# Spreading the score tiles of an attention stage over the eight PSUM banks in another way

## The chip, the cores and the metric

The program runs on one core of a Trainium2 chip. The metric is the device time of one execution in microseconds (us). Five engines matter: TensorE (PE, with its weight loads shown as PEld), VectorE (DVE), ScalarE (ACT), GpSimd (POOL), and SyncE (SP), which here only issues DMA transfers. TensorE writes its results into PSUM, which has eight banks of 2 KB a partition; ACT and DVE read them from there.

## The reference

A transformer block over 2048 tokens of width 576, with a modulation computed from one vector `c`. What matters here is its first half:

```python
h = layernorm(x) * (1 + ca) + sa
q, k, v = split(h @ wqkv)                  # 32 heads of 18
scores = q @ k.T * 18 ** -0.5              # a query sees itself and the 255 keys before it
o = softmax(scores) @ v
x = x + ga * (o @ wo)
h = layernorm(x) * (1 + cb) + sb
x = x + gb * mixer_and_mlp(h)              # token shift with w1, w2; then w3 (576 to 4608), gelu, w4
```

## The kernel before

Nearly every product is made exact by splitting an operand into a rounded high part and the low part that is left; a tile's high part is copied out of PSUM by ACT, and DVE or POOL subtracts it to get the low part.

The work has three phases that follow each other. Phase A holds layernorm, q/k/v projection, attention and the first 12 tiles of the output projection. Phase B holds the last four of these and the token mixer, phase C the MLP. Phases B and C allocate their own PSUM pool and are untouched in it.

All steps of a phase are put on a time line by hand (`play` sorts them by a due time). In phase A the order of PE and POOL is exactly this order (`manual_schedule`); the order on ACT, DVE and SP is left to the framework's scheduler. A PSUM tile names a tag; tiles of one tag share `bufs` banks, and a new tile waits until the last reader of the bank's old tile is done. In phase A the eight banks are shared out as: `sc` 3, `st` 2, `tr` 2, `av` 1.

The steps of phase A that the change and the prediction touch:

- **Row transposes** (`tr` inside `ln`). A normalized row tile of 128 tokens is transposed in two PSUM tiles, `hT..pa` (512 columns, line 283) and `hT..pb` (the last 64 features, line 286). ACT applies scale and shift (lines 291, 293) and makes the high part (294, 295); POOL makes the low part of `pa` (296), DVE that of `pb` (297).
- **Projections** (`vproj`, `qproj`). 14 matmuls each into a tile from `dense`, which walks through `sc` and `st` in turn. q and k go to DRAM (`qkh`, `qkl`) and come back as unit loads.
- **Attention units.** There are 32: 4 chunks `c` of 8 heads, 4 groups `g` of 512 queries, 2 halves `hq` of 4 heads. `uload` brings a unit's q and k into one of four buffers `U` by 12 DMAs on SP (line 399). `s2` computes row-wise scores, 16 tiles `sc` (425), and DVE takes the row maximum of each (432); the maxima are transposed (446, tile `mT` in `tr`), copied by ACT (448) and written into the unit's `U` by two DMAs on SP (450). `s3` computes the scores again, transposed, with the maximum taken off: 16 tiles `X` in `st` (12 where g is 0), each one or two matmuls (475) and a mask matmul (476); ACT takes the exponential of each (482). Twice a unit the products with v follow (497, one `av` bank), and their result is copied (502), transposed (509, tile `oT` in `tr`), divided (511, 515) and written out (517). On PE, `s3` of one unit and `s2` of a later one alternate tile by tile.
- **Output projection** (`s4`, in phase A for g below 3 during chunk 3). A row tile is loaded, transposed by `split9` (lines 64 to 74: `oTT..pa` and `oTT..pb`, both in `tr`; DVE's low parts at 70 and 74), multiplied by `wo` in two halves (676, tiles `po` in `tr`), added (677), and normalized on DVE and POOL.
- **Modulation vectors** (`spill`, line 202): eight small matmul groups into `tr` during chunks 1 and 2.

Of the kernel before, what the change touches and what calls it, by code (L numbers as in the profile page):

```python
# [8 lines left out]
F32 = mybir.dt.float32  # L9
F32R = mybir.dt.float32r  # L10
# [40 lines left out]
class Kern:  # L51
# [11 lines left out]

    def split9(self, row, L, cs, name):
        nc = self.nc
        pa = self.ps.tile([P, KC, P], F32, tag="tr", name=name + "pa", bufs=self.b_tr)
        for k in range(KC):
            nc.tensor.transpose(pa[:, k, :], row[:, k * P:(k + 1) * P], self.ident)
        nc.scalar.copy(L[:, 0:KC, cs], pa)
        nc.vector.tensor_tensor(out=L[:, KC:2 * KC, cs], in0=pa, in1=L[:, 0:KC, cs].bitcast(F32), op=ALU.subtract)  # L70
        pb = self.ps.tile([TAIL, P], F32, tag="tr", name=name + "pb", bufs=self.b_tr)
        nc.tensor.transpose(pb, row[:, KC * P:D], self.ident)
        nc.scalar.copy(L[:TAIL, 2 * KC, cs], pb)
        nc.vector.tensor_tensor(out=L[TAIL:, 2 * KC, cs], in0=pb, in1=L[:TAIL, 2 * KC, cs].bitcast(F32), op=ALU.subtract)
# [52 lines left out]
    def phase_a(self):  # L127
# [8 lines left out]
        qkl = self.dr.tile([2 * D, S], F32, name="qkl")  # L136
        NGA = 4
        with ExitStack() as st:
            self.ps = self.pool(st, "psA", space=PSUM)
# [25 lines left out]
            def cond():  # L165
                fm["x"] = pp.tile([P, 12 * P], F32, tag="P", name="modx", bufs=self.b_p)
                cr = fm["x"][0:KC + 1, 9 * P:10 * P]
                sr = fm["x"][0:KC + 1, 10 * P:11 * P]
                nc.vector.memset(cr, 0.0)
                nc.sync.dma_start(cr[0:KC, :], self.c[0:1, 0:KC * P].rearrange("o (k p) -> (o k) p", p=P))  # L170
                nc.sync.dma_start(cr[KC:KC + 1, 0:TAIL], self.c[0:1, KC * P:])
                nc.scalar.activation(sr, cr, AF.Exp, scale=-1.0)
                nc.vector.tensor_scalar(sr, sr, 1.0, None, op0=ALU.add)
                nc.vector.reciprocal(sr, sr)
                nc.vector.tensor_tensor(out=sr, in0=sr, in1=cr, op=ALU.mult)
                pc = self.ps.tile([P, KC + 1], F32, tag="tr", name="pc", bufs=self.b_tr)
                nc.tensor.transpose(pc, sr, self.ident[0:KC + 1, 0:KC + 1])
                nc.vector.tensor_copy(silu, pc)

            def modvec(v):  # L180
# [17 lines left out]
                def spill():  # L198
                    for hf in range(2):
                        cs = slice(hf * 288, (hf + 1) * 288)  # L200
                        pm = self.ps.tile([P, 288], F32, tag="tr", name=f"pm{v}{hf}", bufs=self.b_tr)
                        nc.tensor.matmul(pm, ones, acc[0][:, cs], start=True, stop=True)
# [48 lines left out]
            def mod_tr():  # L251
                pc = self.ps.tile([P, 3, P], F32, tag="tr", name="pc2", bufs=self.b_tr)
                for j in range(2):
# [10 lines left out]
            def ln(t):  # L264
# [13 lines left out]
                def tr():  # L278
# [3 lines left out]
                    x, L, cs = xrows[t], hT[g], slice(i * P, (i + 1) * P)  # L282
                    pa = self.ps.tile([P, KC, P], F32, tag="tr", name=f"hT{t}pa", bufs=self.b_tr)
                    for k in range(KC):
                        nc.tensor.transpose(pa[:, k, :], x[:, k * P:(k + 1) * P], self.ident)
                    pb = self.ps.tile([TAIL, P], F32, tag="tr", name=f"hT{t}pb", bufs=self.b_tr)
                    nc.tensor.transpose(pb, x[:, KC * P:D], self.ident)
# [49 lines left out]

            banks_p = [("sc", self.b_sc), ("st", self.b_st), ("sc", self.b_sc), ("st", self.b_st), ("sc", self.b_sc)]
            turn = [0]
# [72 lines left out]
            def s2(c, g, hq):  # L412
# [29 lines left out]
                def fin2():  # L442
                    mr = box[1]
                    pm = self.ps.tile([8, 4, P], F32R, tag="tr", name=f"mT{c}_{g}_{hq}", bufs=self.b_tr)
                    for i in range(4):
# [8 lines left out]
            def s3(c, g, hq):  # L454
# [50 lines left out]
                def fin2():  # L505
                    avs = abox[1]
                    pt = self.ps.tile([P, 4, 4, 32], F32, tag="tr", name=f"oT{c}_{g}_{hq}", bufs=self.b_tr)
                    for i in range(4):
# [140 lines left out]
    def s4(self, g, i):  # L649
# [10 lines left out]
        def tr():  # L660
            box["T"] = rp.tile([P, 2 * KC + 1, P], F32R, tag="oT", name=f"oT{t}", bufs=1)
            self.split9(box["o"], box["T"], slice(0, P), f"oTT{t}")

        def wo(hf):
            def f():
                T, x = box["T"], box["x"]
                cs = slice(hf * 288, (hf + 1) * 288)
                tag = "tr" if g < 3 else "mm"
                po = self.ps.tile([P, 288], F32, tag=tag, name=f"po{t}_{hf}", bufs=self.b_tr if g < 3 else self.b_mm)
                pl = []  # L670
# [93 lines left out]
    def phase_bc(self):  # L764
        nc = self.nc
        with ExitStack() as st:
            cp = self.cp = self.pool(st, "bc")
            self.ps = self.pool(st, "psB", space=PSUM)
            self.gb = cp.tile([P, D], F32, name="gb")
            nc.sync.dma_start(self.gb, self.modd[5].to_broadcast([P, D]))  # L770
# [298 lines left out]
    ng = NG  # L1069
    b_mm, b_sc, b_st, b_tr, b_av = 1, 3, 2, 2, 1  # L1070
    b_row, b_p, b_xn, b_gf, b_x1 = 5, 4, 2, 2, 4
# [39 lines left out]
```

## Time and profile before

| | |
|---|---|
| median of 3 runs | 1833.42 us (1831.3 to 1837.96) |
| profiled execution, its time | 1839.11 us |
| its span in the profile | 1837.0 us |
| PE busy over the span | 1761.6 us (96%) |
| DVE, ACT, POOL busy | 984.2, 611.1, 385.6 us |
| row transposes and projections | about 19 to 236 us |
| attention, with output projection from 600 us on | about 206 to 735 us |
| phase B, then phase C | about 735 to 1837 us |

A row of a timeline reads: start, duration, engine, line, operation, output<-inputs, shape, count; in brackets how long the engine stood idle before it and what ended that. A row of the waits reads: who, where, whom it waited for; total us, times, longest. PE's durations are modelled and overlap, so the starts carry more than the lengths. A row of the windows reads: the stretch, its length, busy time (and count) of PE, PEld, DVE, ACT, POOL, the granted share of the TensorE clock, the DMA engines' busy share, GB/s.

### The profile page before, as it was taken

What the parts mean: (1) busy time and instruction counts of PE and PEld (TensorE: products, weight loads), DVE (VectorE), ACT (ScalarE), POOL (GpSimd) and SP (SyncE); (2) the same over time, 40 slices, a digit from 0 to 9 for tenths busy, and PEclk for the clock granted to TensorE, in tenths of its full rate; (3) what the DMA queues carried; (4) which work ended last, traced back from release to release, by engine and by line L of the source; (5) the groups of instructions that cost most, each with busy time, mean ns of one, the idle gap of its engine ahead of it and who ended that gap; (6) DMA issues with size and microseconds to landing.
All of it is one profiled execution on the core that took longest, in us unless ns stands there. A gap on an engine that the chain in (4) does not pass through costs nothing.

```text
span 1837.0 us, 30267 instructions
## 1 busy us (share of the span) xinstructions
PE 1761.6 (96%) x11700; PEld 1508.9 (82%) x11700; DVE 984.2 (54%) x2670; ACT 611.1 (33%) x1292; POOL 385.6 (21%) x376
## 2 busy tenths in 40 slices
PE   6999899999998988999999999999999999999999
PEld 4898666666665777899889999999999999999998
DVE  4401377777776796787744444444444444444433
ACT  5622146556665444435311112111121111111111
POOL 4420220022003011110323332333222111111100
PEclk7999999999998999999999999999999999999999
DMA  6433433354344455642311111111111000000002
GB/s 183 138 104 133 168 108 94 101 134 125 97 110 119 153 176 188 226 144 70 100 48 39 54 47 34 54 54 41 47 34 35 14 28 28 28 28 28 1 1 103
DMA packets 97904, 156.88 MB, mean 85 GB/s; under 512 B 11226, under 2 KB 40670, under 8 KB 97762
## 3 DMA queue, kind: packets, MB, share of 16 engines
q1 hardware_dynamic: 87394, 136.09, 24.9%
q10 hardware_dynamic: 10368, 18.88, 2.8%
q8 instruction: 92, 1.51, 0.3%
q14 instruction: 50, 0.41, 0.1%
HBM read 107.06 MB, written 47.20 MB: 84 GB/s over the span
## 4 chain that ended last, share of the span: by engine, by line
PE 55%; DVE 2%; POOL 1%; issue 0%; DMA 0%; ACT 0%; SPq 0%; DVEq 0%; ACTq 0%; POOLq 0%
PE p L1039 25%; PE p L1010 21%; PE pg L851 2%; PE w L904 2%; PE p L1012 2%; PE p L1011 2%; DVE x L905 0%; DVE xr L99 0%; PE po L676 0%; DMA r<-in_B_w_dram 0%; DVE G L869 0%; POOL CW L994 0%; DVE xm L778 0%; DVE G L856 0%; DVE LNT L70 0%
## 5 line engine op out<-in xcount | busy, mean ns | idle before, releaser
L1039 PEld LDWEIGHTS p<-CW,Gc 128*128 128x128 f32 x3456 | 474.4, 188 | 16.2 <-DVE Gc L1021 3.7
L1039 PE MATMUL p<-CW,Gc 128*128 128x288 f32 x3456 | 482.8, 296 | 3.4 <-DVE Gc L1021 3.4
L1010 PE MATMUL p<-LNT,CW 128*128 128x512 f32 x1728 | 419.8, 392 | 0.0
L1010 PEld LDWEIGHTS p<-LNT,CW 128*128 128x128 f32 x1728 | 316.8, 188 | 58.7
L1018 ACT ACTIVATE gfc<-p 128x512 f32<-128x512 f32 x144 | 86.1, 598 | 735.7 <-PE p L1012 735.7
L432 DVE CUSTOM_DVE_ANT_0 sc<-sc,mask 128x384 f32<-128x384 f32 (+2 forms) x512 | 264.5, 552 | 120.7 <-PE sc L425 114.9
L1043 DVE TENSOR_TENSOR acc<-p,acc 128x288 f32<-128x288 f32 x340 | 153.3, 455 | 317.5 <-PE p L1039 310.7
L482 ACT ACTIVATE P<-X 128x384 f32<-128x384 f32 x480 | 228.4, 489 | 155.2 <-PE X L476 149.3
L425 PE MATMUL sc<-U 126*128 126x384 f32 (+2 forms) x512 | 201.4, 409 | 15.1 <-DMA U<-qkl 9.2
L475 PE MATMUL X<-U 128*128 128x384 f32 (+2 forms) x704 | 193.8, 330 | 10.2 <-ACT P L482 7.7
L475 PEld LDWEIGHTS X<-U 128*128 128x128 f32 x704 | 124.3, 193 | 61.0 <-ACT P L482 32.2
L1043 DVE TENSOR_TENSOR accw<-p,accw 128x288 f32<-128x288 f32 x204 | 89.9, 453 | 130.0 <-PE p L1039 128.7
L476 PE MATMUL X<-maskb,identb 128*128 128x256 bf16 x480 | 137.5, 286 | 0.0
L1021 DVE TENSOR_TENSOR Gc<-gfc,Gc 128x512 fp32r<-128x512 f32 x144 | 127.7, 887 | 4.5
L370 PE MATMUL pq<-hT,Wq 128*128 128x512 f32 x504 | 123.2, 403 | 0.1
L425 PEld LDWEIGHTS sc<-U 126*128 126x128 f32 x512 | 100.4, 201 | 23.7 <-DVE m L432 9.3
L370 PEld LDWEIGHTS pq<-hT,Wq 128*128 128x128 f32 x504 | 96.0, 192 | 23.0 <-DVE m L432 0.5
L990 POOL TENSOR_TENSOR CW<-r,CW 128x1024 fp32r<-128x1024 f32 x17 | 41.3, 2428 | 281.5 <-DVE CW L988 281.5
L497 PE MATMUL av<-P,V 128*32 128x256 f32 (+2 forms) x1472 | 95.0, 390 | 0.0
L1020 ACT CAST Gc<-gfc 128x512 fp32r<-128x512 f32 x144 | 89.4, 621 | 4.6
L994 POOL TENSOR_TENSOR CW<-r,CW 128x1152 fp32r<-128x1152 f32 x17 | 46.4, 2727 | 158.3 <-DVE CW L993 158.3
L476 PEld LDWEIGHTS <-identb 128*128 128x128 bf16 x480 | 46.4, 97 | 35.0 <-issue 14.6
(1075 smaller groups left out, 1971.5 us busy)
## 6 DMA issues: line engine op xcount, KB each, us to landing
U<-qkh SPq DMA_DIRECT2D x160, 72.0 KB
U<-qkh SPq DMA_DIRECT2D x96, 108.0 KB
r<-in_B_w_dram SPq DMA_DIRECT2D x18, 576.0 KB
qkh<-hl ACTq DMA_DIRECT2D x36, 256.0 KB
qkl<-hl ACTq DMA_DIRECT2D x36, 256.0 KB
r<-in_B_w_dram SPq DMA_DIRECT2D x18, 512.0 KB
U<-qkl SPq DMA_DIRECT2D x80, 72.0 KB
U<-qkl SPq DMA_DIRECT2D x48, 108.0 KB
```

The lines of the kernel that those rows point to most:

```text
L370: nc.tensor.matmul(pq, a, b, start=(n == 0), stop=(n == len(pl) - 1))
L425: nc.tensor.matmul(sc[:, lo:], QZ[:KR, q, i * P:(i + 1) * P], KZ[:KR, j, i * P + lo:(i + 3) * P], start=True, stop=True)
L432: nc.vector.tensor_tensor_reduce(out=sc[:, lo:], in0=sc[:, lo:], in1=mask[:, lo:], scale=1.0, scalar=-3e38, op0=ALU.add, op1=ALU.max, accu ...
L475: nc.tensor.matmul(X[:, x0:x0 + nb, :].rearrange("p a b -> p (a b)"), KZ[:, j, kb * P:(kb + 1) * P], QZ[:, q, qb * P:(qb + nb) * P], start ...
L476: nc.tensor.matmul(X[:, 0::2, :], self.identb, mk, start=False, stop=True)
L482: nc.scalar.activation(Pb[b][:, q, :], Xb[b, q].rearrange("p a b -> p (a b)"), AF.Exp, scale=SCALE)
L497: nc.tensor.matmul(abox[0][32 * q:32 * q + 32, q0:q0 + w], V[4 * g + kb][:, hv:hv + 32], Pb[b][:, q, p0:p0 + w], start=(first and n == 0), ...
L1010: nc.tensor.matmul(pg, W3[:, ws, fs], L[:, xs, :], start=(i == 0), stop=False)
L1020: nc.scalar.copy(Gh, gf)
L1021: nc.vector.tensor_tensor(out=Gl, in0=gf, in1=Gh.bitcast(F32), op=ALU.subtract)
L1039: nc.tensor.matmul(po, a, w, start=(i == 0), stop=(i == len(seq) - 1))
L1043: nc.vector.tensor_tensor(out=acc[t][:, cs], in0=po, in1=acc[t][:, cs], op=ALU.add)
```

## The change

The eight banks of phase A are shared out anew: `sc` 3, `st` 3, `tr` 1, `av` 1.

- `X` tiles rotate over three banks instead of two.
- The maxima `mT` and the outputs `oT`, and the two small transposes of the start, share one `tr` bank.
- Row transposes: `pa` goes to `tr` and `av` in turn, `pb` takes a `dense` bank.
- `dense` walks `sc`, `st` alternately (before: `sc`, `st`, `sc`, `st`, `sc`).
- `spill` uses `sc`.
- Output projection for g below 3: `split9` puts `pa` in `sc` and `pb` in `st`, the two halves of `po` go to `sc` and `st`. In phase B all stays as it was.

No instruction is added or removed and the hand-made order of steps is the same.

```diff
-    def split9(self, row, L, cs, name):
+    def split9(self, row, L, cs, name, tags=("tr", "tr")):
-        pa = self.ps.tile([P, KC, P], F32, tag="tr", name=name + "pa", bufs=self.b_tr)
+        pa = self.ps.tile([P, KC, P], F32, tag=tags[0], name=name + "pa", bufs=self.nb[tags[0]])
...
-        pb = self.ps.tile([TAIL, P], F32, tag="tr", name=name + "pb", bufs=self.b_tr)
+        pb = self.ps.tile([TAIL, P], F32, tag=tags[1], name=name + "pb", bufs=self.nb[tags[1]])
...
+        self.nb = {"sc": self.b_sc, "st": self.b_st, "tr": 1, "av": 1}
...
-                        pm = self.ps.tile([P, 288], F32, tag="tr", name=f"pm{v}{hf}", bufs=self.b_tr)
+                        pm = self.ps.tile([P, 288], F32, tag="sc", name=f"pm{v}{hf}", bufs=self.b_sc)
...
-                    pa = self.ps.tile([P, KC, P], F32, tag="tr", name=f"hT{t}pa", bufs=self.b_tr)
+                    pa = self.ps.tile([P, KC, P], F32, tag=("tr", "av")[t % 2], name=f"hT{t}pa", bufs=1)
...
-                    pb = self.ps.tile([TAIL, P], F32, tag="tr", name=f"hT{t}pb", bufs=self.b_tr)
+                    pb = dense([TAIL, P], f"hT{t}pb")
...
-            banks_p = [("sc", self.b_sc), ("st", self.b_st), ("sc", self.b_sc), ("st", self.b_st), ("sc", self.b_sc)]
+            banks_p = [("sc", self.b_sc), ("st", self.b_st)]
...
-                    pm = self.ps.tile([8, 4, P], F32R, tag="tr", name=f"mT{c}_{g}_{hq}", bufs=self.b_tr)
+                    pm = self.ps.tile([8, 4, P], F32R, tag="tr", name=f"mT{c}_{g}_{hq}", bufs=1)
...
-                    pt = self.ps.tile([P, 4, 4, 32], F32, tag="tr", name=f"oT{c}_{g}_{hq}", bufs=self.b_tr)
+                    pt = self.ps.tile([P, 4, 4, 32], F32, tag="tr", name=f"oT{c}_{g}_{hq}", bufs=1)
...
-            self.split9(box["o"], box["T"], slice(0, P), f"oTT{t}")
+            self.split9(box["o"], box["T"], slice(0, P), f"oTT{t}", ("sc", "st") if g < 3 else ("tr", "tr"))
...
-                tag = "tr" if g < 3 else "mm"
-                po = self.ps.tile([P, 288], F32, tag=tag, name=f"po{t}_{hf}", bufs=self.b_tr if g < 3 else self.b_mm)
+                tag = ("sc", "st")[hf] if g < 3 else "mm"
+                po = self.ps.tile([P, 288], F32, tag=tag, name=f"po{t}_{hf}", bufs=self.nb[tag])
...
-    b_mm, b_sc, b_st, b_tr, b_av = 1, 3, 2, 2, 1
+    b_mm, b_sc, b_st, b_tr, b_av = 1, 3, 3, 2, 1
```

More of the change, by code (lines that the diff above doesn't have):

```diff
@@ L175, in cond @@
                 nc.vector.tensor_tensor(out=sr, in0=sr, in1=cr, op=ALU.mult)
-                pc = self.ps.tile([P, KC + 1], F32, tag="tr", name="pc", bufs=self.b_tr)
+                pc = self.ps.tile([P, KC + 1], F32, tag="tr", name="pc", bufs=1)
                 nc.tensor.transpose(pc, sr, self.ident[0:KC + 1, 0:KC + 1])
@@ L251, in mod_tr @@
             def mod_tr():
-                pc = self.ps.tile([P, 3, P], F32, tag="tr", name="pc2", bufs=self.b_tr)
+                pc = self.ps.tile([P, 3, P], F32, tag="tr", name="pc2", bufs=1)
                 for j in range(2):
@@ L768, in phase_bc @@
             self.ps = self.pool(st, "psB", space=PSUM)
+            self.nb = {"tr": self.b_tr, "mm": self.b_mm}
             self.gb = cp.tile([P, D], F32, name="gb")
```

## The prediction

> **What bounds the kernel now.** I read the page first, then the windows by stage, then the waits of PE and PEld, then the timeline of single attention units.
>
> ```profile
> span 1837.0 us, 30267 instructions
> PE 1761.6 (96%) x11700; PEld 1508.9 (82%) x11700; DVE 984.2 (54%) x2670; ACT 611.1 (33%) x1292; POOL 385.6 (21%) x376
> ```
> ```profile
> 17.00:42.00 25.00, 17.21 (x90) 14.96 (x91) 15.01 (x38) 19.55 (x53) 11.60 (x16) 0.64 0.47 140
> 277.70:290.90 13.20, 13.11 (x113) 9.03 (x112) 9.98 (x36) 8.55 (x19) 0.00 (x0) 1.00 0.29 88
> ```
>
> PE bounds the program as a whole: 96%, more than any other engine. What can be won lies in phase A, where the change is, and a microsecond won on PE there moves everything behind it, because phases B and C start when PE reaches them. The second window is one plain attention unit of 13.20 us. PE looks full in it (13.11), but its lengths are modelled and overlap; the weight loads are busy for 9.03 only, DVE for 9.98, ACT for 8.55. No engine is truly full, so the unit's length is made of waits between them. What PE and its weight loads wait for from 238 us, where the transposed scores begin, to 735 us, where phase A ends:
>
> ```profile
> PE oT L509 <- DVE oT L70: 10.6, 6, 3.6
> PE X L475 <- ACT P L482: 7.7, 8, 2.4
> PE sc L425 <- DMA U<-qkl: 6.2, 8, 1.4
> PE sc L425 <- DMA U<-qkh: 1.9, 2, 1.6
> ```
> ```profile
> PEld X L475 <- ACT P L482: 32.2, 106, 2.6
> ```
>
> The reader is to see three kinds. `X` waits for an exponential, which means for one of the two `st` banks: 7.7 us at the matmuls and 32.2 us in 106 pieces at the weight loads, which go ahead of them. `oT` waits for a `tr` bank that `split9` of the output projection holds: 10.6 us in 6 pieces. And `sc` waits for a unit's load from DRAM: 8.1 us in 10 pieces. The change touches the first two kinds and not the third.
>
> **The change part by part.** It removes and adds no instruction and no transfer, so each term is a wait. The rows come from the profiled execution (1839.11 us, span 1837.0), which lies 5.7 us above the median of 1833.42 us; I take the gain in microseconds off the median.
>
> *Third `st` bank, plain units.* Here is half a unit, first PE, then ACT:
>
> ```profile
> 317.27 0.50 PE L475 MATMUL X<-U 128*128 128x128 f32 x2
> ...
> 322.40 0.44 PE L475 MATMUL X<-U 128*128 128x384 f32 x1
> ...
> 323.19 1.51 PE L497 MATMUL av<-P,V 128*32 128x256 f32 x32
> ```
> ```profile
> 317.99 0.96 ACT L482 ACTIVATE P<-X 128x384 f32<-128x384 f32 x2
> 319.19 1.03 ACT L482 ACTIVATE P<-X 128x384 f32<-128x384 f32 x2 [0.24 <-PE X L476]
> 320.70 0.91 ACT L482 ACTIVATE P<-X 128x384 f32<-128x384 f32 x2 [0.49 <-PE X L476]
> 321.85 0.98 ACT L482 ACTIVATE P<-X 128x384 f32<-128x384 f32 x2 [0.24 <-PE X L476]
> 323.06 0.49 ACT L482 ACTIVATE P<-X 128x384 f32<-128x384 f32 x1 [0.23 <-PE sc L425]
> ```
>
> An exponential ends 1.2 us after its `X` has started (317.27 to 317.99, and half of the 0.96). Two banks so allow a step each 0.6 us. Nine exponentials, hence nine `X`, lie between 317.27 and 322.40, which is 5.13 us or 0.64 a step, and ACT idles 0.24 + 0.49 + 0.24 + 0.23 = 1.20 us in it. Three banks allow a step each 0.4 us, and ACT then sets the pace with 0.49. One of the gaps, 0.49, stands after the transpose of `oT` that is put between two steps, and I leave it; the other three, 0.71 us, I take as gained here. In the other half of a unit ACT has gaps like this one:
>
> ```profile
> 383.77 0.49 ACT L482 ACTIVATE P<-X 128x384 f32<-128x384 f32 x1 [0.18 <-PE X L476]
> ```
>
> There are two such, 0.36 us at most, and I take almost nothing of them, since the products with v wait for the last exponential in any case. A plain unit gives 0.75 us; at most 1.20 + 0.36 = 1.56. Chunks 0 to 2 have 18 units with g above 0. DVE is not the next limit: its 9.98 us fit into 12.4. What is late next is the load of a later unit:
>
> ```profile
> 380.36 0.48 PE L446 MATMUL mT<-identr,mr 128*8 128x128 f32 x4
> ...
> 391.87 0.41 PE L425 MATMUL sc<-U 126*128 126x384 f32 x1 [0.54 <-DMA U<-qkl]
> ...
> 394.45 0.49 PE L446 MATMUL mT<-identr,mr 128*8 128x128 f32 x4
> ```
> ```profile
> 381.61 1.23 SPq L450 DMA_DIRECT2D U<-ms  x2
> ...
> 386.59 0.31 SPq L399 DMA_DIRECT2D U<-qkl  x1
> ```
>
> This is a ring. The transpose of the maxima at 380.36 lets SP write them at 381.61; queued behind that write SP issues the rest of a later unit's load, the last of it at 386.59; the load ends the wait of `sc` at 391.87, 5.3 us after; and 2.6 us later comes the next `mT`. The ring takes 14.1 us, no wait for an `st` bank is part of it, and the third bank shortens none of its parts. Where it binds, a quicker `X` only makes `sc` wait longer for the load. It shows in 10 waits; units whose load lands just before its use, which no row counts, would join them. I take half of the 18 units as held: 9 x 0.75 = 7 us. Bounds: 18 x 1.56 = 28 us if it holds none; and, below nothing, a loss of 18 x 0.49 = 9 us if the maxima's copy on ACT, whose order is planned anew, falls one exponential later and so lengthens the ring.
>
> *Row transposes in three tags.* Eight times `pb` of a row tile waits until `pb` of the tile before is read. The first and the last of the eight by size, and the rows around the first projection:
>
> ```profile
> PE hT3pb L287 <- DVE hT L297: 1.7, 1, 1.7
> ...
> PE hT5pb L287 <- DVE hT L297: 0.5, 1, 0.5
> ```
> ```profile
> 24.69 2.70 POOL L296 TENSOR_TENSOR hT<-x,hT 128x512 fp32r<-128x512 f32 x2
> ```
> ```profile
> 30.26 8.03 PE L356 MATMUL pv<-Wv,hT 128*128 128x288 f32 x42
> ```
>
> The eight make 8.6 us, about half of it before 30 us. The projection at 30.26 stands on PE behind `hT3pb`, and its own operand is complete when the first of POOL's two low parts ends, 24.69 + 1.35 = 26.0 us. It can start 4 us earlier. The later waits interrupt projections and give the other 4 us. Against this, `hT0pa` waits about 0.5 us for the only `tr` bank, and ACT, busy for 19.55 of 25 us here, may set the start. I take 7 us; bounds 0, if ACT holds it all, and 9. `pb` in a `dense` bank costs nothing: 14 matmuls of a projection (8.03 us for three such) run while it is read, and six banks rotate. Without that cover each of 16 `pb` would cost up to the 1.7 us above, 27 us; I exclude this end, because that is today's wait with a rotation of two.
>
> *One `tr` bank for `mT` and `oT`; `spill` in `sc`.* Nothing: the two transposes come in turn, once each in 13.2 us, and their readers follow at once (381.61 is 1.25 us after 380.36, the copy included). If they did meet, 0.5 us in each of 32 units, 16 us, is the upper end. `spill`'s eight tiles take a step's 0.5 us at most, 4 us.
>
> *Output projection in the score banks.* The wait for `tr` goes, 10.6 us:
>
> ```profile
> 613.28 0.66 PE L509 MATMUL oT<-ident,avs 128*128 128x128 f32 x4 [1.29 <-DVE oT L70]
> ...
> 615.41 1.75 PE L676 MATMUL po<-Wom,oT 128*128 128x288 f32 x12
> ```
> ```profile
> 613.26 0.28 DVE L74 TENSOR_TENSOR oT<-oTT1pb,oT 64x128 fp32r<-64x128 f32 x1
> ```
>
> Late next is the projection, which needs what DVE ends at 613.54. Without the wait PE is there at 615.41 - 1.29 = 614.1, still after it, so that all of the 1.29 is gained. In the longest piece, 3.6 us, the readers themselves are late and I let 2 us stay. The price is that `pa` and `po` now take a bank from `sc` and `pb` one from `st` for about 2 us each (the wait of 1.29 and the transposes before it). With two `sc` banks left PE may stop for the maxima; I put 0.3 us on each of the 12 row tiles, 3.6 us, between 0 and 24 (2 us each). Sum: 10.6 - 2 - 3.6 = 5 us, bounds -13 and 10.6.
>
> *Clock.* [...]
>
> ```profile
> 707.60:714.40 6.80, 6.16 (x27) 5.87 (x28) 4.60 (x11) 2.22 (x5) 0.79 (x2) 0.50 0.67 212
> 362.80:366.20 3.40, 3.40 (x12) 2.57 (x10) 2.51 (x9) 1.36 (x3) 2.15 (x2) 0.50 0.08 22
> ```
>
> The first stretch belongs to the wait of 3.6 us for `oT`. I count nothing for it, since 2 us of it may stay; at most it gives 6.8 / 2 = 3.4 us. [...]
>
> Sum: 7 (plain units) + 7 (row transposes) + 5 (output projection) = 19 us, and 1833.4 - 19 = 1814.5 us.
>
> **The rivals.**
>
> *The ring of loads does not bind.* For it: only 10 waits in 32 units. Against it: they are there with two banks already, when `sc` comes later. Then 18 x 1.2 = 22 for the units, 9 for the rows, 7 for the projection and 3 of clock: 41 us, 1793 us.
>
> *The wait only moves.* The products with v start no earlier, because ACT ends its nine exponentials no earlier (323.19 follows them by little), and ACT keeps the start. Then 0 + 4 + 2 = 6 us, 1827 us, which can't be told from no change. Against it speak ACT's own gaps. [...]
>
> *Slower: the ring grows.* If the maxima's copy on ACT is planned behind two more exponentials, 2 x 0.49 us enter the ring in the 24 units with g above 0: 23.5 us more, nothing gained in the units, 12 us gained elsewhere, 1845 us. It decides from one exponential on (12 against 12). For it: SP holds the later load behind line 450, which waits for that copy. Against it: today the write stands only 1.25 us behind its transpose.
>
> **How the numbers follow.** Forecast 0.47 (its own range 1806 to 1823), ring not binding 0.20, only moved 0.20, slower 0.13. A measurement of this kernel tells about 0.5%, 9.2 us, from no change. Faster than 1824.2 are the forecast and the first rival, 0.66 with a little left for misjudged sizes; the second rival is 0.21 with it, slower 0.13. The range 1796 to 1836 cuts about half of the first rival and most of the last.
>
> **What would show it.** Right: `X <- ACT P` falls to a few us and ACT's gaps inside a half unit close; `sc <- DMA U` grows from 8.1 towards 15 us; plain units take 12.4 to 13.2 us; the `hT..pb` waits vanish and the first `pv` starts near 26 us; `oT <- DVE oT` vanishes, and a smaller wait stands at line 676 or 425. The prediction is wrong if units stay at 13.2 us with no wait for U, if `sc <- DVE m` takes the place of the `X` waits, if `mT` and `oT` wait for each other, or if line 450 comes later behind its transpose.

## The result, and the profile after

| | kernel before | kernel changed |
|---|---|---|
| median of 6 runs each | 1836.88 us (1831.3 to 1838.2) | 1823.68 us (1820.41 to 1828.73) |
| ratio | 1 | 0.9927, 95% interval 0.9912 to 0.9942 |
| span of the profiled execution | 1837.0 us | 1821.2 us |
| mean granted clock | 0.982 | 0.982 |

The change makes the kernel 13 us faster by the medians and 15.8 us between the two spans; 19 us were forecast. The 1823.7 us lie inside the range of 1796 to 1836 and 9 us above the forecast of 1814.5; 3.5 of these 9 us come from the kernel before, whose median over six runs is that much above the 1833.42 us from which the forecast was taken. A second series of the changed kernel, on another chip, gave 0.9913 (0.9897 to 0.9929), so the change is worth about 14.5 us, or 0.8%.

The waits of PE and of its weight loads in the changed kernel, over the stage from the first transposed scores to the end of phase A (230 to 717 us); columns: who waited, for whom, total us, times, longest.

```profile
PE sc L426 <- DMA U<-qkl: 11.0, 16, 1.8
PE X L476 <- ACT P L483: 7.6, 7, 2.9
PE sc L426 <- DVE mr L440: 3.5, 4, 1.2
PE sc L426 <- DMA U<-qkh: 3.4, 3, 1.7
PE po L677 <- DVE m L433: 2.8, 7, 0.5
PE sc L426 <- DVE m L433: 2.2, 5, 0.8
```
```profile
PEld X L476 <- ACT P L483: 9.9, 11, 3.1
```

Against the rows of before: `oT <- DVE oT` (10.6 us) is gone, and a smaller wait stands at line 677 instead. At the weight loads `X <- ACT P` fell from 32.2 us in 106 pieces to 9.9 in 11. The matmuls' own wait stayed as large (7.7 before, 7.6 now): 6.0 us of it, where the kernel before has 3.6, stand between 540 and 562 us, where ACT in both kernels also copies the output weights. And `sc <- DMA U` grew from 8.1 to 14.4 us. The bank wait made room for the load's wait. The waits of `sc` for DVE's row maxima grew as well, which the prediction had named as a sign of being wrong: over units 1 to 23 from 1.4 to 4.6 us at the matmuls, and from 8.7 to 22.8 us at the weight loads. They are not a limit of their own: with the loads queued earlier (a_load_early, below) 0.3 and 2.8 us of them are left.

The next two windows are two plain units of the changed kernel: stretch, length, busy time and count of PE, PEld, DVE, ACT, POOL, granted clock, DMA share, GB/s.

```profile
283.60:296.40 12.80, 12.14 (x114) 8.77 (x112) 9.69 (x36) 8.32 (x19) 0.00 (x0) 1.00 0.41 111
309.20:320.60 11.40, 11.40 (x114) 8.69 (x112) 8.32 (x36) 8.03 (x19) 0.00 (x0) 1.00 0.33 95
```

Units 1 to 22 hold 17 units with g above 0, taken from the first `X` of one to that of the next. Ten of them look like the first window, 12.6 to 13.6 us (in the kernel before twelve took 13.0 to 13.6), four took 14.0 to 15.9 (before five, 14.1 to 16.4), and three look like the second, 11.4 us. All three stand in group 3, behind which the smaller loads of a group 0 come; the two such units of chunk 1 took 12.7 and 13.3 us, so the smaller load alone doesn't free a unit. In a free unit ACT's gaps are closed:

```profile
309.61 2.04 ACT L483 ACTIVATE P<-X 128x384 f32<-128x384 f32 x4
312.13 2.25 ACT L483 ACTIVATE P<-X 128x384 f32<-128x384 f32 x5 [0.49 <-PE X L477]
315.96 0.91 ACT L483 ACTIVATE P<-X 128x384 f32<-128x384 f32 x2 [1.58 <-PE X L477]
316.76 0.56 ACT L449 CAST ms<-mT 8x512 fp32r<-8x512 f32 x1
317.23 2.05 ACT L483 ACTIVATE P<-X 128x384 f32<-128x384 f32 x5
```

The row transposes gave their time at the start. The first projection stood at 30.26 us; now it follows `hT3pb` at once:

```profile
26.42 0.42 PE L288 MATMUL hT3pb<-ident,x 128*64 128x128 f32 x1
26.50 4.69 PE L357 MATMUL pv<-Wv,hT 128*128 128x288 f32 x23
```

And some of the gain is lost again at one place that the prediction did not look at, the head of phase B. The second row tile of that phase is loaded late, behind weight pieces and stores on SP, and PE stands still for it. First PE, then SP:

```profile
716.59 0.66 PE L951 MATMUL xnT0pa<-ident,xn 128*128 128x128 f32 x4 [0.70 <-DVE xr L678]
717.09 0.27 PE L953 MATMUL xnT0pb<-ident,xn 128*64 128x128 f32 x1
722.13 1.09 PE L951 MATMUL xnT1pa<-ident,xn 128*128 128x128 f32 x4 [4.77 <-DMA xn<-xnd]
```
```profile
713.86 1.89 SPq L755 DMA_DIRECT2D rw<-in_B_w_dram  x4
716.20 0.34 SPq L691 DMA_DIRECT2D hbd<-xr  x1
716.64 0.38 SPq L680 DMA_DIRECT2D xp<-xr  x1
717.18 0.33 SPq L772 DMA_DIRECT2D gb<-modd  x1
717.56 0.51 SPq L797 DMA_DIRECT2D xn<-xnd  x1
```

The same load and the same transpose in the kernel before, whose last `X` starts at 724 us:

```profile
728.82 0.41 SPq L795 DMA_DIRECT2D xn<-xnd  x1
```
```profile
736.78 0.66 PE L949 MATMUL xnT1pa<-ident,xn 128*128 128x128 f32 x4 [1.34 <-DVE T L806]
```

With the start of the first `X` of each attention unit as a mark, the trace splits the time as follows. "Units 1 to 23" runs from the first `X` of unit 1 to that of unit 23, "last chunk" from the first `X` of unit 24 to the last one, "head of B" from there to the first product of the gate `pg`. Two units are left out of the columns: 0, in which `sc` waits 2.9 us for a load before and 2.8 us in the changed kernel, and 23, in which ACT also copies the output weights (34.4 us together before, 36.6 in the changed kernel). The ratios are to the kernel before on the same chip.

| kernel | first `X` at | units 1 to 23 | last chunk | head of B | ratio (95%) |
|---|---|---|---|---|---|
| before | 237.8 | 292.0 | 159.9 | 14.0 | 1 |
| changed | 230.0 | 285.4 | 153.0 | 18.9 | 0.9927 (0.9912 to 0.9942) |
| changed, again | 231.3 | 283.5 | 154.5 | 18.5 | 0.9913 (0.9897 to 0.9929) |
| b_rows_only | 231.1 | 292.3 | 157.0 | 14.0 | 0.9961 (0.9949 to 0.9974) |
| b_proj_only | 237.2 | 288.4 | 157.6 | 13.3 | 0.9991 (0.9981 to 1.0) |
| b_load_early | 238.7 | 292.2 | 166.3 | 20.1 | 1.0056 (1.004 to 1.0072) |
| a_two_st | 229.2 | 290.2 | 158.2 | 14.1 | 0.9947 (0.9931 to 0.9962) |
| a_rows_old | 238.1 | 287.7 | 151.6 | 18.7 | 0.9952 (0.9934 to 0.9969) |
| a_load_early | 231.2 | 274.0 | 159.1 | 18.5 | 0.9887 (0.9865 to 0.9909) |
| a_early_plain | 231.5 | 276.9 | 149.4 | 18.4 | 0.9877 (0.9863 to 0.989) |
| a_ms_other_queue | 232.4 | 277.0 | 177.5 | 14.5 | 0.9963 (0.9951 to 0.9976) |
| a_ms_act_plain | 230.4 | 274.8 | 152.6 | 18.8 | 0.9845 (0.9826 to 0.9863) |
| a_row_load_act | 230.8 | 283.0 | 150.5 | 14.5 | 0.9888 (0.9873 to 0.9904) |
| a_early_and_row | 232.8 | 275.7 | 150.7 | 15.0 | 0.9826 (0.9805 to 0.9848) |

From the first row to the second: 7.8 us less up to the first `X`, 6.6 less in units 1 to 23, 6.9 less in the last chunk, 2.2 more in units 0 and 23, and 4.9 more in the head of B; 14.2 us in all, and 1.6 us more lie behind that. Two rows of the same stage of the same code differ by up to 4 us (292.0 and 288.4 for units 1 to 23 in `before` and `b_proj_only`, whose code there is the same), so a single column is good to a few microseconds, and only differences that several rows repeat are used below. The granted clock explains this spread, by estimate. In units 1 to 23 it was at half speed for 6.8 us in `before`, 6.8 in b_rows_only, 0 in b_proj_only and 3.4 in a_two_st; less half of these times, as an estimate of what they cost, the four rows are 288.4 to 288.9. The estimate is taken from line 497 in `before`, where 32 products with v take 2.79 us at 376.58, with 0.50 granted, and 1.51 us at 310.11, with 1.00.

### The profile page after: what moved, and what is told of

Its sections match the earlier page's. It is cut to its first block, busy times and chain, and to the rows that moved or that the text cites. A ratio compares the mean times of both kernels' runs of the same rounds, so it can differ in the third digit from the quotient of the medians.

```text
span 1821.2 us, 30288 instructions
## 1 busy us (share of the span) xinstructions
PE 1744.1 (96%) x11700; PEld 1503.8 (83%) x11700; DVE 979.7 (54%) x2670; ACT 605.8 (33%) x1292; POOL 386.1 (21%) x376
## 3 DMA queue, kind: packets, MB, share of 16 engines
q8 instruction: 92, 1.51, 0.3%
## 4 chain that ended last, share of the span: by engine, by line
PE 56%; DVE 2%; POOL 0%; DMA 0%; issue 0%; ACT 0%; SPq 0%; POOLq 0%; ACTq 0%; DVEq 0%
PE p L1041 25%; PE p L1012 21%; PE pg L853 2%; PE w L906 2%; PE p L1014 2%; PE p L1013 2%; DVE x L907 0%; PE po L677 0%; DVE xr L99 0%; DMA r<-in_B_w_dram 0%; DVE G L871 0%; POOL CW L996 0%; DVE xm L780 0%; DVE LNT L70 0%; DVE G L858 0%
## 5 line engine op out<-in xcount | busy, mean ns | idle before, releaser
L483 ACT ACTIVATE P<-X 128x384 f32<-128x384 f32 x480 | 223.9, 489 | 148.6 <-PE X L477 143.4
L426 PE MATMUL sc<-U 126*128 126x384 f32 (+2 forms) x512 | 205.5, 415 | 29.8 <-DMA U<-qkl 13.9
L476 PE MATMUL X<-U 128*128 128x384 f32 (+2 forms) x704 | 182.6, 317 | 8.2 <-ACT P L483 7.6
L476 PEld LDWEIGHTS X<-U 128*128 128x128 f32 x704 | 128.7, 194 | 37.9 <-issue 26.1
L477 PEld LDWEIGHTS <-identb 128*128 128x128 bf16 x480 | 46.7, 97 | 38.7 <-issue 22.8
```

The lines of the kernel that those rows point to most:

```text
L426: nc.tensor.matmul(sc[:, lo:], QZ[:KR, q, i * P:(i + 1) * P], KZ[:KR, j, i * P + lo:(i + 3) * P], start=True, stop=True)
L476: nc.tensor.matmul(X[:, x0:x0 + nb, :].rearrange("p a b -> p (a b)"), KZ[:, j, kb * P:(kb + 1) * P], QZ[:, q, qb * P:(qb + nb) * P], start ...
L477: nc.tensor.matmul(X[:, 0::2, :], self.identb, mk, start=False, stop=True)
L483: nc.scalar.activation(Pb[b][:, q, :], Xb[b, q].rearrange("p a b -> p (a b)"), AF.Exp, scale=SCALE)
```

## The experiments

The names of the kernels begin with `a_` where the changed kernel is altered, and with `b_` where the kernel before is.

**The third bank taken away, the rest kept** (a_two_st).

```diff
-    b_mm, b_sc, b_st, b_tr, b_av = 1, 3, 3, 2, 1
+    b_mm, b_sc, b_st, b_tr, b_av = 1, 3, 2, 2, 1
```

> The changed kernel with two banks instead of three for the transposed scores; the eighth bank stays unused, everything else as changed. My sum gave the third bank 7 us, the traces of before and after show about 4.3 us over the plain units: 1827 to 1831 us, waits for the exponentials back near 30 us on the weight load, units 13.0-13.5 us. Rival (the third bank only moves the wait from the exponentials to the load): 1822 to 1826 us. Second rival (it is worth the whole change): 1835 us or more.

Measured: 1829.8 us, ratio 0.9947. The waits came back where the theory put them, here over units 1 to 23 of this kernel (the weight loads' wait for exponentials there is 20.1 us, 84 times, in the kernel before, and the changed kernel has none):

```profile
PE sc L426 <- DMA U<-qkl: 3.9, 6, 1.2
```
```profile
PEld X L476 <- ACT P L483: 19.8, 84, 0.5
```

No unit with g above 0 took less than 13.0 us any more. By the ratios the third bank is worth 0.0020 against the first series of the changed kernel and 0.0034 against the second, 4 to 6 us net; the interval of the first series overlaps this kernel's, that of the second does not. In the table it is worth more than that, 5 to 7 us in units 1 to 23 and about 4 to 5 in the last chunk, and it costs about 4.6 us in the head of B. (In the last chunk the projection's tiles in `st` share the two banks here.) Neither rival (nothing; the whole change) holds.

**The row transposes put back** (a_rows_old), **and put into the kernel before alone** (b_rows_only).

```diff
-                    pa = self.ps.tile([P, KC, P], F32, tag=("tr", "av")[t % 2], name=f"hT{t}pa", bufs=1)
+                    pa = self.ps.tile([P, KC, P], F32, tag="tr", name=f"hT{t}pa", bufs=1)
...
-                    pb = dense([TAIL, P], f"hT{t}pb")
+                    pb = self.ps.tile([TAIL, P], F32, tag="av", name=f"hT{t}pb", bufs=1)
```

> The changed kernel with the row transposes of the first stage (512-wide part and 64-row part) back in one two-bank rotation, over the two banks that now hold only the 512-wide part; everything behind as changed. If the row transposes' places gave 7.5 to 7.9 us, as the start of the first transposed scores shows: 1829 to 1832 us, first value projection back near 30 us, and the waits of the 64-row part for its bank back. Rival (only the 3.8 us up to the first value projection hang on it, the rest on six dense banks in even rotation instead of five): 1826 to 1828 us.

In the kernel before, `pa` then turns alone over the two `tr` banks:

```diff
-                    pb = self.ps.tile([TAIL, P], F32, tag="tr", name=f"hT{t}pb", bufs=self.b_tr)
+                    pb = dense([TAIL, P], f"hT{t}pb")
```

> The kernel before with one half of the second part alone: the 64-row part of a row transposition goes to the dense banks, and the 512-wide part alternates between the two transposition banks; the transposed scores keep two banks and the output projection its old place. If the row transposes' gain is theirs alone: first value projection near 26.5 us, the first transposed scores 5 to 8 us earlier (230 to 233 us), total 1829 to 1833 us, ratio 0.995 to 0.997. Rival (half of the gain was the even rotation of six dense banks, which this kernel does not have): first transposed scores 3 to 4 us earlier, total 1833 to 1836 us.

Measured: 1830.1 us (ratio 0.9952) and 1832.0 us (0.9961), both where the theory put them. The first projection, first with the transposes put back, then with them alone:

```profile
30.17 1.07 PE L357 MATMUL pv<-Wv,hT 128*128 128x288 f32 x3
```
```profile
26.09 5.18 PE L356 MATMUL pv<-Wv,hT 128*128 128x288 f32 x30
```

The table's first column has two groups and nothing between them: 237.2 to 238.7 us in the four kernels with the old row transposes, 229.2 to 232.8 in the ten with the new ones, means 238.0 and 231.1. This part gives 6.9 us, whichever kernel it stands in. The even rotation of six dense banks is not needed for it: the kernel before has the rotation of five, and gains as much.

**The output projection alone in the kernel before** (b_proj_only). The rotations stay at three `sc`, two `st` and two `tr`.

```diff
...
-            self.split9(box["o"], box["T"], slice(0, P), f"oTT{t}")
+            self.split9(box["o"], box["T"], slice(0, P), f"oTT{t}", ("sc", "st") if g < 3 else ("tr", "tr"))
...
-                tag = "tr" if g < 3 else "mm"
+                tag = ("sc", "st")[hf] if g < 3 else "mm"
...
```

> The kernel before with the third part of the change alone: the output projection's row transposes and products in the score banks (three for the scores, two for the transposed ones), all else as before. My sum gave this part 5 us; the traces of before and after show 6.9 us less over units 24 to 31 with the third bank in it, and two banks instead of three showed 5.2 us more there. Theory (the part gives by itself what is left, with its own banks freed): 1833 to 1837 us, ratio 0.996 to 0.999. Rival (without the third bank the score banks collide with the projection): 1840 us or more, with new waits of the transposed scores for the residual row's addition.

Measured: 1833.4 us beside 1835.6 of the kernel before, ratio 0.9991 with an interval that ends at 1.0. The waits over its last chunk, from the second unit on, show why so little is left. Two rows of the kernel before, then the first three of this one:

```profile
PE oT L509 <- DVE oT L70: 9.6, 5, 3.6
...
PE X L475 <- ACT P L482: 1.2, 2, 0.8
```

```profile
PE X L476 <- ACT P L483: 6.6, 13, 0.7
PE X L476 <- DVE xr L678: 1.2, 2, 1.0
PE oTT0pa L68 <- DMA or<-od: 1.1, 1, 1.1
```

`oT` no longer waits. But `pb` and one half of `po` now hold a bank of the two that the transposed scores have, and these wait 6.6 us for an exponential, where it was 1.2, and 1.2 us for the residual row there. In the changed kernel the waits of `X` for exponentials are 1.7 us in the same units:

```profile
PE X L476 <- ACT P L483: 1.7, 3, 0.8
```

So the two parts belong together. With two banks the move of the projection shows no gain in this chunk: 157.6 us and 158.2 (a_two_st) with it, 159.9 and 157.0 (b_rows_only) without. With the third bank behind it the chunk takes 153.0 and 154.5. A kernel with the third bank and the projection left in `tr` was not run, so how much of this the bank would give without the move is open.

**The loads queued earlier, in both kernels** (a_load_early, b_load_early). One number moves all twelve loads of a unit ahead of the write of the maxima behind which eight to ten of them stood on SP; the order of PE's and POOL's instructions in the changed kernel stays the same.

```diff
-                        ev.append((tb - self.u_ld, uload(c, g, hq)))
+                        ev.append((tb - (1.0 if u > 1 else self.u_ld), uload(c, g, hq)))
```

> The changed kernel with one number altered: the twelve loads of a unit's q and k (line 400) are queued half a pair of units earlier, so that on SP all twelve stand ahead of the row of maxima (line 451) behind which eight to ten of them stand now. Ring theory (a plain unit's length is now set by that order of the queue, not by the score banks): the units fall from 12.7-13.4 us towards the 11.4 us that three units without a late load already show, 18 units by 0.8 to 1.5 us, total 1797 to 1810 us, and the waits of the score matmul for its load (13.9 us at 17 places) fall under 4 us. Rival (the loads come just in time because PE is at its own pace; the wait only changes its name): 1819 to 1827 us, units unchanged. Second rival (the maxima's row now lands late behind the loads, and the transposed scores wait for it): slower, 1828 us or more.

> The kernel before (two banks for the transposed scores) with the same earlier place of the unit's loads and nothing else. If the bank wait bound the units before, and the loads stood close behind it: 1830 to 1838 us, units still 12.8-13.5 us, and the wait of the transposed scores' weight load for the exponentials stays near 32 us. If the loads' ring alone bound them in both kernels: the same gain as in the changed kernel, 1812 to 1822 us.

Measured: 1819.5 us (0.9887) in the changed kernel, and 1849.1 us (1.0056) in the kernel before. Both totals miss what was expected, by 9.5 and 11 us on the slow side. They hide two opposite effects, so the windows over units 1 to 23 come first; `before`, `b_load_early`, `changed`, `a_load_early`, in the columns of the windows above:

```profile
252.90:544.90 292.00, 282.71 (x2383) 194.36 (x2383) 214.43 (x800) 178.22 (x377) 27.98 (x27) 0.99 0.40 107
```
```profile
254.10:546.30 292.20, 281.24 (x2382) 196.09 (x2380) 215.37 (x800) 178.80 (x377) 28.12 (x27) 0.98 0.39 110
```
```profile
246.50:531.90 285.40, 265.98 (x2383) 190.81 (x2382) 209.15 (x800) 173.80 (x377) 28.01 (x27) 0.98 0.41 109
```
```profile
246.80:520.80 274.00, 258.17 (x2383) 188.01 (x2383) 209.11 (x800) 174.87 (x377) 28.11 (x27) 0.99 0.42 116
```

With two banks the earlier loads change nothing (292.0 and 292.2). With three they take 11.4 us off. So two limits lie one behind the other, and the second shows only when the first is gone. That the banks are the first limit is seen in b_load_early: no wait of `sc` for a load is left there, and still no unit with g above 0 takes less than 13.0 us. Two of its rows over these units:

```profile
PE X L475 <- DMA U<-ms: 8.1, 4, 2.7
```
```profile
PEld X L475 <- ACT P L482: 20.9, 87, 0.5
```

The waits for loads over these units, first `changed`, then `a_load_early`:

```profile
PE sc L426 <- DMA U<-qkl: 9.4, 14, 1.8
...
PE sc L426 <- DMA U<-qkh: 1.8, 2, 1.2
```
```profile
PE X L476 <- DMA U<-ms: 11.8, 9, 2.6
PE X L476 <- DMA U<-qkl: 2.1, 1, 2.1
PE sc L426 <- DMA U<-qkl: 0.5, 1, 0.5
PE sc L426 <- DMA U<-qkh: 0.4, 1, 0.4
```

With early loads the odd units with g of 1 or 2 take 11.8 to 12.0 us and four of five with g of 3 take 11.4, while the even ones with g of 1 or 2 take 12.5 to 14.6: the write of the maxima (`U<-ms`) now waits its turn behind the loads, which is the second rival, in 9 places. What spoils the totals lies elsewhere: in the last chunk both kernels lose 5 to 6 us with early loads, and the kernel before another 6 in the head of B. There SP also carries the rows and weights of the output projection, and the framework's scheduler (the planner) set its whole order anew, and the orders of ACT and DVE changed there too.

**Early loads in chunks 0 to 2 only** (a_early_plain). All engines but SP keep the changed kernel's order.

```diff
-                        ev.append((tb - self.u_ld, uload(c, g, hq)))
+                        ev.append((tb - (1.0 if 1 < u < 12 else self.u_ld), uload(c, g, hq)))
```

> The changed kernel with the earlier loads for the units of chunks 0 to 2 only; in the last chunk, where the output projection's rows share SP, the loads keep the place they have in the changed kernel. With all units early the trace showed 11.4 us less over units 1 to 23 and 6 us more over units 24 to 31. Theory (the two effects are apart): units 1 to 23 near 274 us, units 24 to 31 near 155 us, total 1809 to 1814 us, a ratio of 0.983 to 0.987 to the kernel before. Rival (what the early units give is taken back at the last chunk whatever its loads do, since it waits for the output weights): 1816 to 1820 us.

Measured: 1811.3 us, ratio 0.9877, a little above the 0.983 to 0.987 expected. Units 1 to 23 kept most of the gain (276.9), and the last chunk lost nothing (149.4). The rival, 1816 us or more, is excluded.

**The write of the maxima on ACT's queue** (a_ms_other_queue), **and there in chunks 0 to 2 only** (a_ms_act_plain). This separates the two kinds of transfer instead of turning their order round.

```diff
-                        nc.sync.dma_start(QZ[KR + n:KR + n + 1, :, :].bitcast(F32), ms[4 * n:4 * n + 4, :].bitcast(F32))
+                        nc.scalar.dma_start(QZ[KR + n:KR + n + 1, :, :].bitcast(F32), ms[4 * n:4 * n + 4, :].bitcast(F32))
```

> The changed kernel with the row of maxima (line 451) issued from ACT's queue instead of SP's, so that neither the loads stand behind it nor it behind the loads. Ring theory: all plain units fall to 11.4-12 us, the odd and the even ones, units 1 to 23 at 265 to 272 us instead of 285, total 1800 to 1812 us. Rival (ACT has to issue 64 more transfers at some 0.4 us each, and its exponentials become late): units at 12.5 us or more, 1818 to 1830 us, with waits of the transposed scores for the exponentials back.

In the second kernel the queue is `(nc.scalar if c < 3 else nc.sync)`.

> The changed kernel with the row of maxima issued from ACT's queue in chunks 0 to 2 only; in the last chunk it stays on SP, so that DVE's order there is that of the changed kernel. With all chunks on ACT the plain units were all at 12.3-12.6 us, but the last chunk was 22 us longer. Ring theory: units 1 to 23 at 275 to 279 us and units 24 to 31 near 155 us, total 1811 to 1817 us, ratio 0.986 to 0.990. Rival (the last chunk's loss came from what the transfers left on ACT before it, not from its own): 1822 us or more.

Measured: 1827.5 us (0.9963), where the rival put it, and 1809.1 us (0.9845), a little better than expected. Units 1 to 23 took 277.0 and 274.8 us, as with early loads, though not the 265 to 272 expected of the first: the plain units are nearly all alike at 12.3 to 12.9 us, and the loads' waits gave way to these (a_ms_act_plain):

```profile
PE X L476 <- ACT P L483: 7.9, 16, 0.7
PE X L476 <- DMA U<-ms: 4.1, 6, 1.2
PE sc L426 <- DMA U<-qkl: 0.6, 1, 0.6
```

One exponential per unit is late by half a microsecond, 16 times. That is the rival's mechanism: issuing the pair of transfers takes 1.2 us of ACT's queue, as in this row of a_ms_other_queue, 0.6 us each and not some 0.4. With 7.9 us it is too small to make the rival's total.

```profile
301.85 1.20 ACTq L451 DMA_DIRECT2D U<-ms  x2
```

The first kernel loses 23 to 24.5 us in its last chunk against the changed one. 15.2 us of them stand at another wait, the first row there:

```profile
PE po L677 <- DVE oT L70: 15.2, 4, 5.8
```

DVE's order there was planned anew as well, with the subtraction for the projection's operand late. The clock was at half speed for 30.7 us of this chunk, against 7.0 and 8.7 in the changed kernel. In the second kernel DVE keeps its order in this chunk, and the loss is gone.

**The first two row loads of phase B on ACT's queue** (a_row_load_act). The second is the late one.

```diff
-                        nc.sync.dma_start(box[t], self.xnd[t])
+                        (nc.scalar if t < 2 else nc.sync).dma_start(box[t], self.xnd[t])
```

> The changed kernel with the first two loads of the normalised rows for the next stage (line 797, tiles 0 and 1) issued from ACT's queue, where nothing stands ahead of them from 711.5 us on. Theory (the 3.9 us that the changed kernel gives back between the last transposed scores and the first gate product are the second load's place on SP, issued at 717.6 us behind stores and weight loads): first gate product 3 to 4.5 us earlier, total 1820 to 1823 us where the changed kernel has about 1825 on this chip's scale, ratio 0.990 to 0.991. Rival (the first gate product waits for the weights that are loaded there anyway): no change, ratio 0.993.

Measured: 1813.2 us, ratio 0.9888. The second load is issued at 705.77 instead of 717.56, and PE's gap is 1.34 us instead of 4.77:

```profile
705.77 0.33 ACTq L797 DMA_DIRECT2D xn<-xnd  x1
```
```profile
713.50 0.66 PE L951 MATMUL xnT1pa<-ident,xn 128*128 128x128 f32 x4 [1.34 <-DVE T L808]
714.83 0.39 PE L853 MATMUL pg<-T,W1a 128*128 128x256 f32 x1 [0.68 <-ACT T L807]
```

The head of B fell from 18.9 to 14.5 us, what the two-bank kernels have. That is the 4.4 us of the theory. The ratio gives 4.5 to 7 us against the two series of the changed kernel, and 1813.2 us is a larger gain than the 1820 to 1823 us expected. The rest stands in the last chunk (150.5 against 153.0 and 154.5). Most of that goes to the clock, by estimate: it was at half speed there for 3.4 us, against 7.0 and 8.7 in the changed kernel, and half of these differences is 1.8 to 2.7 us. Until ACT issues the first moved load, 1.5 us before the chunk's last `X`, every engine and queue works in the changed kernel's order, so the alteration itself has no hold on the chunk.

**The changed kernel again** (after_again), unaltered, **and both alterations together** (a_early_and_row), the diffs of a_early_plain and a_row_load_act.

> The changed kernel once more, unaltered, beside the three others on the same chip: the scale for them, and a second trace that shows how much of a stage's length changes by itself between executions. Expected ratio to the kernel before 0.991 to 0.994, units 1 to 23 at 283 to 288 us.

> The changed kernel with both alterations that stand for themselves: the earlier loads for the units of chunks 0 to 2, and the first two normalised-row loads issued from ACT's queue. Theory (they lie in different stages and add): the earlier loads gave about 9 us and the row loads about 4 us of the stage's head, so 1804 to 1809 us, ratio 0.983 to 0.986. Rival (they share a cause, SP's backlog, and each takes most of what the other would give): 1810 to 1814 us, no better than either alone.

Measured: 1822.2 us (0.9913) and 1806.0 us (0.9826). They add up: 0.9877 and 0.9888 lie 0.0043 and 0.0032 below the mean of the changed kernel's two ratios, 0.992, and 0.992 less both is 0.9845, inside the interval (0.9805 to 0.9848). This kernel is faster than the one before by 1.7% and than the changed one by 0.9%.

## Why the prediction was right, and its gain 5 us too large

*Row transposes: right.* Forecast 7 us, measured 6.9 as the mean over fourteen traces. Half of it before the first projection, as predicted (30.26 to 26.50).

*Output projection: right in its sum, partly by luck.* Forecast 5 us, measured 6.9 and 5.4 in the last chunk of the two traces. The new wait at `po` was 2.8 us where 3.6 were set. But the term was argued without the third bank, and b_proj_only shows that alone it gives 0 to 3.5 us by the interval of the ratio: the price on `st`, left at a word in the prediction ("`pb` one from `st`"), takes most of it while there are two banks. The third bank pays that price, and for this chunk the prediction had counted no gain of the third bank.

*Third bank in the plain units: right by two errors that cancel.* Forecast 7 us, measured 6.6 between the two traces and 5.8 between the means of four rows each, 290.7 with two banks and 284.9 with three (early loads and the other queue for the maxima left out). The first error is the step "in the other half of a unit ... I take almost nothing of them". The exponentials of that half took 4.03 us before (325.24 to 329.27, with the copy of the maxima among them) and take 3.32 now (315.96 to 319.28), nearly as much gain as in the first half, whose nine took 5.56 us (317.99 to 323.55) and take 4.77 (309.61 to 314.38). A unit without the ring takes 11.4 to 11.9 us, 1.3 to 1.6 less than 13.2 and 13.0; 0.75 was forecast. The second error is the step "I take half of the 18 units as held". Only three of them ran free. With early loads the three banks bring 290.7 to 275.5 (the mean of the three rows with early loads), 15.2 us; without them 9.4 of that are lost, to the ring and, by the next paragraph's estimate, some 2.6 us to the clock. The prediction had the ring right: its rows, its order on SP, that the third bank shortens none of it, and what its wait would be called.

*Clock: nothing counted, and not quite nothing found.* The half-speed stretches of the clock after 40 us sum to 46 us before and to 50 and 58 us in the two traces of the changed kernel; over all fourteen traces they sum to 34 to 61 us. In units 1 to 23 the four rows with two banks have 4.2 us of them on average, the four with three banks 12.0, and the three with three banks and early loads 6.8. With half of a difference as the estimate of what the clock costs, some 4 us of the third bank's gain there went to the clock. That the load waits bring these stretches was not shown. Nor does a run show the 3 us of clock that the first rival adds, or the 3.4 us set as the most for the shorter wait: the stretches grew by 4 and 12 us in sum. The stretch at the old wait of 3.6 us is gone, and another stands at the new wait in phase B:

```profile
719.00:725.80 6.80, 3.21 (x14) 2.78 (x15) 4.89 (x13) 2.28 (x4) 1.91 (x4) 0.50 0.52 144
```

*What was missed: the head of phase B.* The three terms come to 19 us in the table (7.8 + 6.6 + 6.9 = 21.3, less 2.2 in units 0 and 23), as forecast, and 4.9 us of them are lost where phase A ends. The sentence that failed is "a microsecond won on PE there moves everything behind it, because phases B and C start when PE reaches them". Phase B starts when its row tiles are there as well, and the load of the second was issued 12.6 us after PE's last `X` (705.0 to 717.6), in the kernel before 4.9 us after it. Of the kernels with three banks all have 18.4 to 18.9 us there, save those with the row load on ACT and a_ms_other_queue, in which SP carries no write of the maxima (14.5 to 15.0); of the five with two banks four have 13.3 to 14.1. The time from the last `X` to that load tells them apart: 4.9 to 7.7 us in the seven traces with a head of up to 15.0 us, 12.0 to 14.2 in the seven with 18.4 us or more. a_row_load_act shows that the load's place in the queue is the cause. That the planner puts it later is seen in SP's order, with three banks and also in b_load_early with two; why it does was not tried.

Of the rivals, "the ring does not bind" is refuted by the pair of kernels with early loads. "The wait only moves" is refuted in its mechanism, that ACT ends its nine exponentials no earlier (5.56 us before, 4.77 now in a free unit); a wait did move, but to the load, and it kept a part of the gain and not the whole. "The ring grows" did not occur: the write of the maxima stands 1.25 us behind their transpose in both kernels, by the median.

## What to carry to other kernels

The bank added to a rotation was worth what the next limit let through, 5.8 us in units 1 to 23 and 15.2 with the loads queued earlier; look in the trace for transfers that land just before their use, which here showed 8.1 us of waits with two banks and 14.4 with three. When a stage becomes shorter, follow each queue across its end: a load for the next stage that was early enough may now be late, and moving that load to another queue gave back 4.4 us of the 4.9 lost. Where a planner orders the queues, apply an alteration only to the stage that it is for, and compare the orders of all engines before comparing times: the same earlier loads gave 11 us in one stage and cost 5 to 6 in the next. Before a difference of a few microseconds between two traces is explained, look at how long the clock was at half speed in that stage of each.

## What the runs showed of the hardware that was not expected

In the traces of `before` and of the changed kernel each half-speed stretch of the clock after the first 40 us is 3.4 or 6.8 us long (the one at the program's end is cut short), and how long PE stood idle ahead of it does not by itself tell where one comes. In `before` one stands at 376.5 to 379.9 us; in the 3.4 us ahead of it PE was busy for 2.07 us, with gaps of 0.29 us (before 374.86) and 0.95 us (before 376.22). From 681.8 to 685.2 us of the same trace PE was busy for 0.31 us, with gaps of 1.21 us (before 683.02) and 1.89 us (before 685.22), and the granted clock is 1.00 there and up to 688.6.

The same code takes a stage in different times, and in two of three groups of rows the clock, by the estimate above, explains nearly all of it. The kernel before spread over 8 to 10 us in each of its three longer series (1834.1 to 1843.3 in one of them, 15 runs). In units 1 to 23 the time at half speed ranges from 0 to 13.7 us over the fourteen traces. With half of it taken off, the four rows with two banks and unaltered loads, which were 288.4 to 292.3 us, become 288.4 to 288.9, and the three with three banks and early loads, 274.0 to 276.9, become 271.8 to 272.3. The four with three banks and unaltered loads, 283.0 to 287.7, stay as far apart, at 276.2 to 280.9.
